# Late tokens and queries turned by the DMA queue, weight conversions by half tiles, and a new written-out order

## The chip, the core and the metric

The kernel runs on one core of a Trainium2 chip. Its time is device microseconds (us) for one execution of the whole program. The engines are TensorE (PE, with its weight loads PEld), VectorE (DVE), ScalarE (ACT), GpSimd (POOL) and SyncE (SP); each works through its own list of instructions in order and waits for the others by semaphores. SP computes nothing: it issues DMAs, and ACT and POOL issue some as well, between their own instructions.

## What is computed

Block-sparse attention over 4 batches, 8 heads, 768 tokens of width 64, and then an MLP with a PReLU on the 3072 tokens of width 512:

```python
scores = np.matmul(q, k.transpose(0, 1, 3, 2)) / np.sqrt(64)
# blocks of 32 tokens; a query block sees its neighbours, the first and the last block, 3 drawn blocks;
# the first and the last query block see everything
mask = (abs(blk_i - blk_j) <= 1) | (blk_i == 0) | (blk_j == 0) | (blk_i == 23) | (blk_j == 23) | drawn
attn = softmax(np.where(mask, scores, -1e9))
x = (attn @ v).transpose(0, 2, 1, 3).reshape(3072, 512)
h = x @ w_in                                   # 512 x 2048
g = np.maximum(h, 0.0) + alpha * np.minimum(h, 0.0)
out = g @ w_out                                # 2048 x 512
```

The MLP's weights arrive as 64-bit floats and have to be converted on the chip. Products are made with operands split into an fp16 high part and an fp16 low part (three fp16 products stand for one fp32 product).

## The kernel before, in words

**Units.** Batch b has six query tiles t of 128 tokens; tile 5 holds the dense blocks. A unit is one tile with four of the eight heads (c = 0 or 1). A unit makes scores `s` on PE, the exponent `e` (DVE L811 or L825, then ACT), fp16 high and low parts of the probabilities `p` by rows in a buffer `ph`, and SP turns these with DMA transposes (L867, L871) into `pt`; PE then makes the weighted values `a` (L713). Keys are turned the same way (L579).

**Queries and tokens.** Queries (`qf`) are turned on PE: four 128x128 transposes (L508) into PSUM, then a high part by ACT or DVE and a low part by DVE (L444) from PSUM into `qt`. When both units of a tile have their `a`, DVE multiplies by the reciprocal sums (L875, into `xf`), PE turns the tile with four transposes (`emit_x_pe`, L883), and ACT or DVE (L592, L594) and DVE (L899) write the high and low parts into `x`.

**MLP.** Two tiles of x are a chunk of 256 tokens; chunks M0 to M11, of which M6 to M11 belong to batches 2 and 3. An up-product (L1307, 24 matmuls) makes `h`; the activation makes `g`, its high part `gh` and low part `gl`; a down-product (L1368, 12 matmuls) adds into the two `o` tiles. Batch 0 and its first chunk work in fp32 ("wide", L1331, activation at L1337 and L1338). At the end of a chunk ACT scales the two tiles (`emit_out`, L1378) and SP stores them.

**Weights.** A tile f of 128 rows of w_in or w_out is loaded raw into space that is later `wo`'s (or, at the end, into idle buffers `x` and `vr`), and three instructions make fp32 of it: N1 (L1159, DVE), N2 (L1166 on DVE, or a byte move at L1164 on ACT), N3 (L1171, DVE). They work on pairs of tiles (128x1024). After them come scaling and splitting on ACT, DVE and POOL (L436, L446, L447).

**Order.** Every step is recorded as an operation with its dependencies; the string ORDER says, for each place, which operation comes next and on which engine (an operation's number and the letter of its engine). Buffers are given out in the order of that string. Nothing is decided at run time but the waits.

```python
LQW = ({"ACT": 0.45, "SP": 0.35}, {"ACT": 0.45}, {"POOL": 1.0}, {"POOL": 1.0, "ACT": 0.45})[W_ACT]
MAX4 = {"DVE": (0.42, 0), "ACT": 0.65, "POOL": 0.8}
LOW3 = {"DVE": (0.72, 0), "POOL": (0.72, 1.15)}
```

These give the engines that an operation may stand on; LQW is the list for the loads of weights.

Of the kernel before, what the change touches and what calls it, by code (L numbers as in the profile page):

```python
# [18 lines left out]
P = 128  # L19
# [27 lines left out]
W_ACT = 1  # L47
WIDE = 1
TB0, TB1 = ["o", "s"], ["s"]
# [14 lines left out]
01G2aA2eP03V02G00G0AV0EG2kA04G08G2pP09V06V07G33S2ZS2cP3GA3HP2jA0IP2dV2bA2gP2iS2nP2hV0KA0LV3IA32S34A2sS2qA2tA2rS0DG0MV2fA3JG0CA3KG2lP2mA3LG2oA0BV3MG3SP  # L64
35P3ZV3aA36V0NV43S37P38V3hG3iG3DA3jG3kG46G47G48G2uP2vV44P3TV3UA49G3bV2YS3VV2wP3mP3cA2xV2-G3dP2yV0WA3tV3WA3XP4UG3eV3nV4VG4WG45A4FP3YA2+G3uA3vV4sA3oA3pV
39G4MV3wA3xP3qA3+V0OA0SA4GV4HA3yV4IV4NA4XG4vG4ZP4OV0XV4wG4xG4yG5HG3rP5IG5JG4tP0YV4JA4KP4gV4PA4uV3BV4QP4aV3sA2XS3NG3OG0PV0QV4LA3PG3QG52P4hA4iV4AG4bA4cV
3RS5KG4RA0JV4jA4kP4dA4eP59V3lS0RV0qP0rP53V5jG30A5kG5AA5BV3CV54A55V4oV5CA5DP4BG3fP0ZV3gP5EA5MP0TV3zP0UV0VV3-P5gS4ES5NV4CG4lA56A5TV5OA5PV0HG4DG0aA4fV5UA
40V5lG4YA57P5VV41P3AV5hP5QA5mG05G42V0sP0tP0eA5iA5RP5sP3FV4SP4TP4mP7CA0FG0iA5WA65G5SV4nP5bV5XP58A0mA66G0bV0cV5tV5zV0dV4pV4qP67G68G7FG5YV7GG5-A6AP5+V4rA
6WP60A61P0fV0gV6aP0hV0uP1FA5uA1GA0vP5vV7DP0jV6XV6HV0kA6BV6CA0lV1LA6eP0wP31G0nV62A0oV5wA5xP6DV6IA0pV6EA6JV6FP6KA7HG1HV6bV0xP7IG7EA7OP2zG1KA6fV4zG4-G4+G
0yV0zP1IA1JV50G1QA51S6iP5FP0-V0GA6mP7PV7dG5nG1PA7VV5yA5oG5pG5qG1zP6PV5GP7eG7fG6VV7gG7QA7WA7iP7XV7YA7RV7SA1MV7TP1NV1OV5LA5ZP6YA6GA7ZP6jV5aP1-P6qP1RV1SV  # L70
1TV1UA80S6gA1+P7jV6nV6cA0+G10G1VA7UA81P6uP7aA7pV7kA7lV5cV5rS63P1ZA1aA7mA7nP6LP1WV7qA7rV69ABAA82A1XV1YV7oA20P83P6ZG1bV5dP64P1cV1dV1fA6MA6vV6dG7JG8CV84P
# [1449 lines left out]
```

## Time and profile before

| | |
|---|---|
| median of 3 runs | 778.02 us (777.37 to 780.0) |
| the profiled execution | 781.22 us, of which the span of its instructions is 778.5 us |
| PE busy | 727.4 us, 93% |
| DVE busy | 529.8 us, 68% |
| ACT busy | 324.4 us, 42% |
| POOL busy | 490.9 us, 63% |

The profiled execution is one execution of the program with the hardware profiler on; its time is 2.7 us more than its span, and 3.2 us above the median of the three runs without it. Busy time is the time in which an engine has an instruction under way; what the engine waits for is seen in the chain of waits and in the idle time before an instruction.

### The profile page before, as it was taken

How to read it: one execution, taken by the hardware profiler on the slowest of the kernel's cores; microseconds unless marked ns; L12 is line 12 of the kernel's file. 1: busy time of each engine (PE TensorE's matmuls, PEld its weight loads, DVE VectorE, ACT ScalarE, POOL GpSimd, SP SyncE). 2: the span in 40 equal slices, each digit the busy share in tenths (PEclk: the TensorE clock that was granted, in tenths of full speed). 3: DMA queues.
4: the chain of work that ended last, by engine and by line, in shares of the span. 5: the costliest groups of instructions: out<-in, count | busy, mean ns of one | idle time of the engine just before them, and what ended most of it. 6: DMA issues, size and time to landing. Idle time of an engine off the chain costs nothing.

```text
span 778.5 us, 25844 instructions
## 1 busy us (share of the span) xinstructions
PE 727.4 (93%) x10417; PEld 501.2 (64%) x10417; DVE 529.8 (68%) x1240; ACT 324.4 (42%) x765; POOL 490.9 (63%) x854
## 2 busy tenths in 40 slices
PE   4867997899999979999999799999999999999997
PEld 3645875656766656666776467576766677566764
DVE  4776899999748885867857456686676664665321
ACT  2532524565325434455535344355452443352211
POOL 4888676377779864468766576477586786233121
PEclk9987998999999989999999899999999999999999
DMA  9979886746685978967679869657897768345100
GB/s 225 277 192 302 238 213 172 147 90 161 152 184 119 166 151 152 188 137 157 144 210 167 156 131 164 161 109 144 134 202 163 142 130 163 62 89 85 36 1 27
DMA packets 241607, 117.63 MB, mean 151 GB/s; under 512 B 194496, under 2 KB 227920, under 8 KB 241488
## 3 DMA queue, kind: packets, MB, share of 16 engines
q1 hardware_dynamic: 196224, 64.46, 45.1%
q10 hardware_dynamic: 39600, 33.69, 16.2%
q0 software_dynamic: 5664, 17.84, 9.0%
q8 instruction: 81, 1.33, 0.8%
q14 instruction: 38, 0.31, 0.2%
HBM read 71.91 MB, written 12.58 MB: 109 GB/s over the span
## 4 chain that ended last, share of the span: by engine, by line
PE 80%; DVE 8%; issue 5%; POOL 3%; DMA 2%; ACTq 1%; POOLq 1%; ACT 0%; SPq 0%; DVEq 0%
PE o L1368 31%; PE h L1307 29%; PE s L713 7%; PE a L713 6%; DVE wo L1171 1%; PE h L1331 1%; DVE wo L1166 1%; ACTq L464 1%; POOL keys L708 1%; PE s L883 1%; PE s L508 1%; DVE wo L1159 1%; DMA vf<-in_k_dram 1%; DVE e L811 1%; DVE ph L438 1%
## 5 line engine op out<-in xcount | busy, mean ns | idle before, releaser
L1307 PE MATMUL h<-x,wi 128*128 128x256 f16 x2112 | 247.1, 274 | 1.3 <-DVE g L1338 1.3
L1368 PE MATMUL o<-wo,gh 128*128 128x512 f16 x768 | 230.3, 382 | 0.0
L1307 PEld LDWEIGHTS <-wi 128*128 128x128 f16 x2112 | 204.4, 99 | 36.2 <-issue 4.6
L1324 POOL TENSOR_TENSOR gl<-g,gh 128x512 f16<-128x512 f32 x88 | 105.7, 1205 | 158.1 <-ACT gh L1319 149.5
L1368 PE MATMUL o<-wo,gl 128*128 128x512 f16 x384 | 146.3, 381 | 0.0
L708 POOL COPY keys<-keys 128x128 f16 (+1 forms) x480 | 129.8, 319 | 15.4 <-PE s L713 11.3
L818 ACT ACTIVATE e<-e,smalls 128x256 f32<-128x256 f32 x160 | 80.2, 502 | 127.8 <-DVE smalls L811 121.8
L1368 PEld LDWEIGHTS <-gh 128*128 128x128 f16 x768 | 72.6, 99 | 75.4 <-issue 4.8
L1313 DVE SCALAR_TENSOR_TENSOR g<-h,am 128x512 f32<-128x512 f32 x88 | 60.4, 686 | 78.0 <-PE h L1307 60.8
L1319 ACT CAST gh<-g 128x512 f16<-128x512 f32 x88 | 53.7, 612 | 133.6 <-DVE g L1314 96.2
L665 POOL DMA_INDIRECT vr<-scr,vidx x80 | 83.3, 1042 | 24.7 <-issue 16.4
L713 PE MATMUL s<-keys,qt 64*32 64x192 f16 (+5 forms) x2376 | 77.6, 271 | 10.9 <-ACT pt L436 4.7
L811 DVE CUSTOM_DVE_ANT_0 e<-s,bias,smalls 128x256 f32<-128x256 f32 x120 | 54.1, 478 | 25.4 <-PE s L713 22.3
L713 PEld LDWEIGHTS <-pt 128*32 128x32 f16 (+1 forms) x3456 | 48.8, 96 | 30.4 <-issue 23.5
L1368 PEld LDWEIGHTS <-gl 128*128 128x128 f16 x384 | 37.7, 98 | 46.0 <-issue 1.1
L1314 DVE SCALAR_TENSOR_TENSOR g<-h,g 128x512 f32<-128x512 f32 x88 | 60.8, 691 | 3.0
L444 DVE SCALAR_TENSOR_TENSOR ph<-e,ph 128x512 f16<-128x512 f32 (+1 forms) x56 | 50.3, 903 | 11.9 <-ACT ph L436 11.5
L713 PE MATMUL a<-vr,pt 128*32 128x64 f16 (+1 forms) x1760 | 43.2, 205 | 10.2 <-issue 6.1
L447 POOL TENSOR_TENSOR ph<-e,ph 128x512 f16<-128x512 f32 (+1 forms) x36 | 50.7, 1408 | 3.0
L436 ACT ACTIVATE ph<-e 128x512 f16<-128x512 f32 (+1 forms) x66 | 46.2, 706 | 3.6 <-DMA keys<-ph 2.3
L836 ACT ACTIVATE e<-e,smalls 128x768 f32<-128x768 f32 x32 | 29.8, 930 | 40.7 <-DVE smalls L832 40.3
L713 PE MATMUL a<-vn,pt 128*32 128x64 f16 (+1 forms) x1760 | 40.8, 205 | 5.0 <-DMA vn<-scr 4.0
(225 smaller groups left out, 933.7 us busy)
## 6 DMA issues: line engine op xcount, KB each, us to landing
vn<-scr SPq DMA_DIRECT2D x54, 192.0 KB, 4.1
wo<-in_moe_w_in_dram ACTq DMA_DIRECT2D x8, 1024.0 KB, 10.9
wo<-in_moe_w_out_dram ACTq DMA_DIRECT2D x12, 512.0 KB, 4.1
vn<-scr ACTq DMA_DIRECT2D x26, 192.0 KB, 4.1
vf<-in_v_dram SPq DMA_DIRECT2D x14, 256.0 KB, 3.4
vf<-in_k_dram SPq DMA_DIRECT2D x24, 128.0 KB
qf<-in_q_dram SPq DMA_DIRECT2D x12, 256.0 KB, 5.5
scr<-v SPq DMA_DIRECT2D x11, 256.0 KB, 3.0
```

Source lines behind the costliest of these rows:

```text
L447: nc.gpsimd.tensor_tensor(dst, tmp, hi, ALU.subtract)
L665: nc.gpsimd.indirect_dma_start(dst[:n], None, T["scr", b].rearrange("s h a -> s (h a)"), bass.IndirectOffsetOnAxis(ap=vidx[:n, i : i + 1], ...
L708: nc.gpsimd.tensor_copy(kr[:, :, r], kt[:, :, bass.ds(i * HB2, HB2)])
L713: nc.tensor.matmul(dst, lhs, rhs, start=start, stop=False, skip_group_check=True)
L811: nc.vector.tensor_tensor_reduce(e_view(u, h // 2)[:, h % 2, :], T["sp", u, h], bias[:, t], scale=T["cs", b, t][:, c : c + 1], scalar=3.0e ...
L818: nc.scalar.activation(e, e, AF.Exp, bias=T["nm", u, h], scale=-1.0, accum_out=su_of(u, h))
L1307: nc.tensor.matmul(h[:, i, :], win(k, f, ct), x[:, l, ct, :], start=(m == 0), stop=(m == len(terms) - 1))
L1313: nc.vector.scalar_tensor_tensor(g, ph, 0.0, a2, ALU.min, ALU.mult)
L1314: nc.vector.scalar_tensor_tensor(g, ph, GSCALE, g, ALU.mult, ALU.add)
L1319: nc.scalar.copy(T["gh", c, j], g)
L1324: nc.gpsimd.tensor_tensor(T["gl", c, j], g, T["gh", c, j], ALU.subtract)
L1368: nc.tensor.matmul(T["o", c, t], g[:, i, t * P : (t + 1) * P], wout(w, f), start=(f == 0 and m == 0), stop=(f == NF - 1 and m == 2),)
```

## The change

Six things change.

1. Batch 3's six query tiles (`Q_T`) and the twelve x tiles of batches 2 and 3 (`X_T`) are no longer turned on PE. DVE, ACT or POOL writes the high part and DVE or POOL the low part by rows into a `ph` buffer, and SP issues one DMA transpose for each tile.
2. N1, N2 and N3 work on single tiles (128x512) in place of pairs. Of N1 and N3 there are now 32 each (18 before), of N2 15 on ACT and 17 on DVE (4 and 14 before).
3. The first chunk's activation is a Relu with scale -1 on ACT, from PSUM, and two DVE instructions of 128x256 for each up-product, in place of two DVE instructions of 128x512. `emit_alpha` has one instruction more.
4. Loads of weights may be issued by SP as well as by ACT: 16 of 24 now stand on SP.
5. The last three down-products of the last chunk are made by token tile, and tile t = 1's output is scaled and stored in two halves.
6. ORDER is another one: 2535 operations in place of 2480, and most stand elsewhere.

```diff
-W_ACT = 1
+W_ACT = 0
+Q_T = {(3, t) for t in range(6)}
+X_T = {(b, t) for b in (2, 3) for t in range(6)}
...
 ORDER = """
-01G2aA2eP03V02G00G0AV0EG2kA04G08G2pP09V06V07G33S2ZS2cP3GA3HP2jA0IP2dV2bA2gP2iS2nP2hV0KA0LV3IA32S34A2sS2qA2tA2rS0DG0MV2fA3JG0CA3KG2lP2mA3LG2oA0BV3MG3SP
+3DS03V06V08G0IP04V09V05G00G02G01G3wS0BV0AV0FG0DG3GP3FS3NS3RP07G3KP3LV3HA3xP3ES3IP3JV3MA3VA3PP0GA3yV3QV3OS3TP3XA3zG3-G3UA4jS3kA3SA3+G3iA40G46P4kP4LG4lA
...
+    def by_rows(nb):
+        return phs[nb.slot].rearrange("p a b c -> p (a b c)")[:, : 2 * HQ * P]
+
+    def emit_q_n_hi(e, b, t, nb):
+        T["qn", b, t] = by_rows(nb)
+        times(e, T["qn", b, t][:, : HQ * P], T["qf", b, t].rearrange("p h d -> p (h d)"), T["sq", b, t])
+
+    def emit_q_n_lo(e, b, t):
+        src, nat = T["qf", b, t].rearrange("p h d -> p (h d)"), T["qn", b, t]
+        rest(e, nat[:, HQ * P :], src, T["sq", b, t], nat[:, : HQ * P], src)
+
+    def emit_q_t(b, t):
+        T["qt", b, t] = wt("qt", [P, H, P], F16)
+        nc.sync.dma_start_transpose(T["qt", b, t], T["qn", b, t])
...
+    def emit_x_n_hi(e, b, t, nb):
+        T["xn", b, t] = by_rows(nb)
+        src, dst = T["xf", b, t].rearrange("p h d -> p (h d)"), T["xn", b, t][:, : HQ * P]
+        if e == "POOL":
+            nc.gpsimd.tensor_copy(dst, src)
+        else:
+            copy(e, dst, src)
+
+    def emit_x_n_lo(e, b, t):
+        nat = T["xn", b, t]
+        eng_of[e].tensor_tensor(nat[:, HQ * P :], T["xf", b, t].rearrange("p h d -> p (h d)"), nat[:, : HQ * P], ALU.subtract)
+
+    def emit_x_t(b, t):
+        nc.sync.dma_start_transpose(x_part(b, t), T["xn", b, t])
...
+        if (b, t) in X_T:
+            nb = plan.buf("ph")
+            o = plan.op(p - X_UP, MAX4, lambda e: emit_x_n_hi(e, b, t, nb), [o], [nb], [fb])
+            o = plan.op(p - X_UP, {"DVE": (0.7, 0), "POOL": (0, 1.2)}, lambda e: emit_x_n_lo(e, b, t), [o], [], [nb, fb])
+            o_x[b, t] = plan.op(p - X_UP, {"SP": 1.3}, lambda: emit_x_t(b, t), [o], [xbuf[cc]], [nb], dma=1.55)
+            return
...
         nc.vector.tensor_scalar(am1, am0, GSCALE, None, ALU.mult)
+        nc.vector.tensor_scalar(am0, am0, -1.0, None, ALU.mult)
...
-    def emit_n1(name, fs):
-        r, low, d, byte = raw_of(name, fs)
+    def emit_n1(name, fs, i):
+        r, low, d, byte = raw_of(name, fs, i)
         nc.vector.tensor_scalar(d, r, 3, 0x3FFFFFFF, ALU.logical_shift_left, ALU.bitwise_and)
...
-        o = plan.op(p, {"DVE": (0.4 * n, 0)}, lambda: emit_n1(name, fs), o + free, [], use)
-        o = plan.op(p, {"ACT": 1.27 * n, "DVE": (0.65 * n, 0)}, lambda e: emit_n2(e, name, fs), [o], [], use)
-        return plan.op(p, {"DVE": (0.65 * n, 0)}, lambda: emit_n3(name, fs), [o], [], use)
+        last, ld = [], o
+        for i in range(n):
+            o = plan.op(p, {"DVE": (0.4, 0)}, lambda i=i: emit_n1(name, fs, i), (ld if name == "wi" else ld[i : i + 1]) + free, [], use)
+            o = plan.op(p, {"ACT": 1.27, "DVE": (0.65, 0)}, lambda e, i=i: emit_n2(e, name, fs, i), [o], [], use)
+            last = [plan.op(p, {"DVE": (0.65, 0)}, lambda i=i: emit_n3(name, fs, i), [o] + last, [], use)]
+        return last[0]
...
-    def emit_act_wide(j, gb):
-        h = T["h", 0, j]
-        g = T["g", 0, j] = wt(gb.pool, [P, 2, W2], F32)
-        a2 = am0[:, 2 * j : 2 * j + 2].unsqueeze(2).broadcast_to([P, 2, W2])
-        nc.vector.scalar_tensor_tensor(g, h, 0.0, a2, ALU.min, ALU.mult)
-        nc.vector.tensor_tensor(g, h, g, ALU.add)
+    def emit_act_neg(j, gb):
+        T["g", 0, j] = wt(gb.pool, [P, 2, W2], F32)
+        nc.scalar.activation(T["g", 0, j], T["h", 0, j], AF.Relu, scale=-1.0)
+
+    def emit_act_wide(j):
+        h, g = T["h", 0, j], T["g", 0, j]
+        for i in range(2):
+            nc.vector.scalar_tensor_tensor(g[:, i], g[:, i], am0[:, 2 * j + i : 2 * j + i + 1], h[:, i], ALU.mult, ALU.add)
...
+                if c == len(chunks) - 1 and j >= NG - 3:
+                    o = [plan.op(p, {"PE": 1.3}, lambda j=j, t=t: emit_down_half(c, j, t), d + fin[t], [], [hbs[j], lbs[j], obufs[t]]) for t in range(2)]
+                    fin = [[x] for x in o]
+                    continue
```

The order of instructions is shown at three places. The first is the start of DVE's list. `sf`, `bq`, `dd` and `btab` belong to the mask of the drawn blocks, `vpick`, `vrow` and `vidx` to the indices of the gathered values, and `spack` (L365 before, L368 after) packs the block numbers that POOL then reads into its registers. Before:

```order
L321 TENSOR_SCALAR wi<-rawp 1x72
L330 TENSOR_TENSOR dd<-sf,bq 128x15
L331 TENSOR_TENSOR dd<-dd 128x15
...
L409 SCALAR_TENSOR_TENSOR vpick<-vpick,vrow 128x20
L410 TENSOR_SCALAR vidx<-vpick,vrow 128x20
L365 SCALAR_TENSOR_TENSOR spack<-wi 1x30
L594 COPY keys<-s_109 128x4x128
```

After:

```order
L324 TENSOR_SCALAR wi<-rawp 1x72
L368 SCALAR_TENSOR_TENSOR spack<-wi 1x30
L327 TENSOR_SCALAR vpick<-rawp 128x60
L328 MEMSET vpick 32x60
...
L413 TENSOR_SCALAR vidx<-vpick,vrow 128x20
L346 SCALAR_TENSOR_TENSOR dtab<-bcol,sf,dtab 128x24 x3
L333 TENSOR_TENSOR dd<-sf,bq 128x15
...
L612 COPY keys<-s_109 128x4x128
```

The packing moves from behind the mask and the indices to the place directly behind the block numbers; the mask now comes last.

The second place is DVE's list where w_out is converted and the first chunk's activations stand between the conversions. `wo` is w_out's space, `vf_70` a `g` of the first chunk, `h_113` its up-product, `am_153` alpha's table. Before:

```order
L1159 TENSOR_SCALAR wo<-wo 128x1024
L1166 SCALAR_TENSOR_TENSOR wo<-wo 128x1024
L1171 SCALAR_TENSOR_TENSOR wo<-wo 128x1024
L1337 SCALAR_TENSOR_TENSOR vf_70<-h_113,am_153 128x512
L1338 TENSOR_TENSOR vf_70<-h_113,vf_70 128x512
```

After:

```order
L1206 TENSOR_SCALAR wo<-wo 128x512
L1213 SCALAR_TENSOR_TENSOR wo<-wo 128x512
L1218 SCALAR_TENSOR_TENSOR wo<-wo 128x512
L1390 SCALAR_TENSOR_TENSOR vf_70<-vf_70,am_153,h_113 128x256 x2
L829 ISA e_75,smalls<-s_111,bias,cs_140 128x256
...
L1206 TENSOR_SCALAR wo<-wo 128x512 x2
L1213 SCALAR_TENSOR_TENSOR wo<-wo 128x512
L1218 SCALAR_TENSOR_TENSOR wo<-wo 128x512 x2
```

A set of N1, N2, N3 is of half the size and there are twice as many; in the last rows one of two N2 is missing, it stands on ACT. Softmax rows (`e_75`) and activations come between smaller pieces.

The third place is PE's list around the last chunk's second x tile. `a_112` is the weighted values from which that tile is made, `xf_83` the tile, `x_84` and `x_86` the x of the last chunk (before and after), `gh_104`, `gh_103`, `gh_102` high parts of the chunk before. Before:

```order
L713 MATMUL a_112<-v_97,pt_79 128x64
L1307 LDWEIGHTS wi
L1307 MATMUL h_114<-x_86,wi 128x256
...
L883 MATMUL s_111<-ident,xf_83 128x128 x4
L1368 LDWEIGHTS gh_104
...
L1368 MATMUL o_116<-wo,gl_106 128x512
L1307 LDWEIGHTS wi
L1307 MATMUL h_113<-x_84,wi 128x256
```

After:

```order
L731 MATMUL a_112<-v_94,pt_80 128x64
L1420 LDWEIGHTS gh_104
...
L1420 LDWEIGHTS gh_103
...
L1420 LDWEIGHTS gh_102
...
L1357 LDWEIGHTS wi
L1357 MATMUL h_114<-x_86,wi 128x256
```

The four transposes (`s_111<-ident,xf_83`) are gone from PE, and three down-products in place of an up-product, the transposes and a down-product stand between the last weighted values and the first up-product that reads the new tile. Meanwhile the tile goes through DVE, ACT or POOL and then SP, whose list at this place reads, after:

```order
L889 DMA_TRANSPOSE pt_80<-ph_137 128x6x128
L889 DMA_TRANSPOSE pt_79<-ph_137 128x6x128
L922 DMA_TRANSPOSE x_86<-ph_134 128x8x128
L922 DMA_TRANSPOSE x_86<-ph_135 128x8x128
L467 DMA out_dram<-g_88 128x512
```

The two x tiles are turned behind the last transposes of dense probabilities. At the very end of ACT's list (not shown) the two halves of tile t = 1 are scaled first, then tile t = 0, and then ACT issues the store of t = 0.

## Rows read from the trace of the kernel before

**Rows 1.** Windows: length; PE, PEld, DVE, ACT, POOL busy us; clock, DMA share, GB/s.
```profile
0.00:92.00 92.00, 66.92 (x874) 51.03 (x875) 62.31 (x171) 34.98 (x91) 68.34 (x191) 0.91 0.94 246
92.00:148.00 56.00, 47.78 (x692) 37.47 (x691) 54.41 (x91) 23.89 (x49) 35.84 (x26) 0.94 0.74 192
...
430.00:720.00 290.00, 282.72 (x4462) 191.26 (x4447) 184.42 (x461) 121.27 (x290) 177.29 (x290) 0.99 0.71 135
```

**Rows 2.** Chain of waits in the stretch 92 to 148, shares by line.
```profile
by line: DVE wo L1171 20.8%; DVE wo L1166 19.4%; DVE wo L1159 13.9%; issue 9.0%; DVE e L811 6.1%; PE s L713 4.3%; DVE e L825 3.8%; PE a L713 3.4%; DVE xf L875 2.5%; DVE g L1338 2.5%; DVE vf L1337 2.2%; DVE g L1337 2.2%; DVE ph L444 1.7%; DV
```

**Rows 3.** Chain of waits from 448 to 458: start us, us, what.
```profile
448.89 0.44 PE s L883 x4
449.33 2.59 PE o L1368 x12
...
456.53 0.59 PE s L508 x4
```

**Rows 4.** DVE's groups by line and shape, 92 to 148: busy us, mean ns | idle.
```profile
L1171 DVE SCALAR_TENSOR_TENSOR wo<-wo 128x1024 int32<-128x1024 int32 x5 | 11.2, 2250 | 0.2
L1166 DVE SCALAR_TENSOR_TENSOR wo<-wo 128x1024 int32<-128x1024 int32 x5 | 9.6, 1913 | 0.1
L1159 DVE TENSOR_SCALAR wo<-wo 128x1024 int32<-128x1024 int32 x5 | 6.6, 1311 | 0.0
...
L875 DVE TENSOR_TENSOR xf<-a,smalls 128x512 f32<-128x512 f32 x3 | 2.1, 687 | 0.5 <-PE a L713 0.5
...
L899 DVE TENSOR_TENSOR x<-o,x 128x512 f16<-128x512 f32 x2 | 1.4, 682 | 0.0
```

**Rows 5.** DVE timeline from 72: start us, us, instruction.
```profile
72.36 0.68 DVE L1159 TENSOR_SCALAR wi<-wo 128x1024 int32<-128x1024 int32 x1
73.08 1.23 DVE L1166 SCALAR_TENSOR_TENSOR wi<-wo,wi 128x1024 int32<-128x1024 int32 x1
74.34 1.23 DVE L1171 SCALAR_TENSOR_TENSOR wi<-wo,wi 128x1024 int32<-128x1024 int32 x1
```

**Rows 6.** DVE timeline from 141: conversions of single tiles.
```profile
141.46 0.43 DVE L1159 TENSOR_SCALAR wo<-vr 128x512 int32<-128x512 int32 x1
141.80 0.69 DVE L1166 SCALAR_TENSOR_TENSOR wo<-x,wo 128x512 int32<-128x512 int32 x1
```

**Rows 7.** DVE timeline from 87: the first chunk's activation.
```profile
87.89 0.69 DVE L1338 TENSOR_TENSOR g<-h,g 128x512 f32<-128x512 f32 x1
88.50 0.68 DVE L1337 SCALAR_TENSOR_TENSOR g<-h,am 128x512 f32<-128x512 f32 x1
89.22 0.69 DVE L1338 TENSOR_TENSOR g<-h,g 128x512 f32<-128x512 f32 x1
```

**Rows 8.** POOL and DVE timelines from 97: two instructions that run at once.
```profile
97.85 2.00 POOL L447 TENSOR_TENSOR gl<-g,gh 128x512 f16<-128x512 f32 x1
...
98.87 2.06 DVE L1171 SCALAR_TENSOR_TENSOR wo<-wo 128x1024 int32<-128x1024 int32 x1
```

**Rows 9.** SP's transposes of probabilities (line L867): duration min/median/max, time to landing.
```profile
L867 SPq DMA_TRANSPOSE pt<-ph x60: 1231/1258/3727, 237.4 to 674.6; - x60
...
DMA to landing us min/median/max: 3.0/4.8/10.6
```

**Rows 10.** Timeline of the start; start us, us, instruction.
```profile
13.73 0.17 DVE L365 SCALAR_TENSOR_TENSOR spack<-wi 1x30 int32<-1x30 int32 x1
...
17.48 0.65 POOL L708 COPY keys<-keys 128x64 f32 x1
```

**Rows 11.** ACT timeline from 60; in brackets the idle time before and its releaser.
```profile
60.49 4.58 ACTq L464 DMA_DIRECT2D wo<-in_moe_w_in_dram  x1
65.11 0.51 ACT L818 ACTIVATE e<-e,smalls 128x256 f32<-128x256 f32 x1 [4.68 <-issue]
```

**Rows 12.** Timeline of the end.
```profile
773.53 1.27 ACT L1378 ACTIVATE g<-o,smalls 128x512 f32<-128x512 f32 x2 [5.61 <-PE o L1368]
```

**Rows 13.** PE timeline, 437 to 444.
```profile
442.92 0.27 PE L713 MATMUL a<-vr,pt 128*32 128x64 f16 x5 [5.17 <-issue]
```

More of the change, by code (lines that the diff above doesn't have):

```diff
@@ L68 @@
[L68 to L71, printed above, removed]
@@ L114 @@
+d7Pd4Vd5Ad6Gd8PdCPd9VdAAdBGdDPdHPdEVdFAdGGdIPdMPdJVdKAdLGdNPdRPdSPdOVdPAdQGdTPdUPdVPdWPdZAdbAdXAdaSdcSdYA
 """
@@ L1166, in emit_n2, with emit_n3 @@
             nc.vector.scalar_tensor_tensor(d, low, 29, d, ALU.logical_shift_right, ALU.bitwise_or)
-        T["mask", name, fs] = 7 - (1 << 30) if e == "ACT" else -(1 << 30)
-    def emit_n3(name, fs):
-        r, low, d, byte = raw_of(name, fs)
-        nc.vector.scalar_tensor_tensor(d, r, T["mask", name, fs], d, ALU.bitwise_and, ALU.bitwise_or)
+        T["mask", name, fs, i] = 7 - (1 << 30) if e == "ACT" else -(1 << 30)
+    def emit_n3(name, fs, i):
+        r, low, d, byte = raw_of(name, fs, i)
+        nc.vector.scalar_tensor_tensor(d, r, T["mask", name, fs, i], d, ALU.bitwise_and, ALU.bitwise_or)
     def emit_w_sq(name, fs, tb, first, last):
@@ L1357, in emit_fs, with emit_down @@
         nc.vector.reciprocal(T["fs", b], t1)
-    def emit_down(c, j):
+    def emit_down(c, j, ts=(0, 1)):
         if j == 0:
@@ L1365, in emit_down @@
             f = 2 * j + i
-            for t in range(2):
+            for t in ts:
                 for m, (g, w) in enumerate(((gh, 0), (gh, 1), (gl, 0))):
@@ L1374, in emit_down, with emit_down_half @@
                     )
+    def emit_down_half(c, j, t):
+        emit_down(c, j, (t,))
     def emit_out(c, t):
@@ L1378, in emit_out, with emit_out_half, emit_store, emit_store_half @@
         nc.scalar.activation(T["ob", c, t], T["o", c, t], AF.Copy, scale=T["fs", chunks[c][0]])
-    def emit_store(e, c, t):
+    def emit_out_half(e, c, t, x):
+        if x == 0:
+            T["ob", c, t] = wt("g", [P, DM], F32)
+        y = slice(x * DM // 2, (x + 1) * DM // 2)
+        times(e, T["ob", c, t][:, y], T["o", c, t][:, y], T["fs", chunks[c][0]])
+    def emit_store(e, c, t, y=slice(0, None)):
         b, i = chunks[c]
         for a, z, s in q_rows(b, 2 * i + t):
-            load(e, out[b * S + s : b * S + s + z - a], T["ob", c, t][a:z])
+            load(e, out[b * S + s : b * S + s + z - a, y], T["ob", c, t][a:z, y])
+    def emit_store_half(e, c, t, x):
+        emit_store(e, c, t, slice(x * DM // 2, (x + 1) * DM // 2))
     o_fs = {}
@@ L1413, in moe @@
                     last = o
-                    o = plan.op(p - MOE_BOOST, {"DVE": 1.47}, lambda j=j, gb=gb[j]: emit_act_wide(j, gb), [o, o_al], [gb[j]], [hb])
+                    o = plan.op(p - MOE_BOOST, {"ACT": 0.6}, lambda j=j, gb=gb[j]: emit_act_neg(j, gb), [o], [gb[j]], [hb])
+                    o = plan.op(p - MOE_BOOST, {"DVE": 0.85}, lambda j=j: emit_act_wide(j), [o, o_al], [], [gb[j], hb])
                 else:
@@ L1432, in moe @@
             ob = plan.buf("g")
-            o = plan.op(stop - MOE_BOOST, {"ACT": 0.58}, lambda t=t: emit_out(c, t), [downs[-1], o_fs[b]], [ob], [obuf])
+            if fin[t] and t == 1:
+                for x in range(2):
+                    o = plan.op(stop - MOE_BOOST, {"ACT": 0.38, "DVE": 0.4}, lambda e, x=x: emit_out_half(e, c, 1, x), fin[1] + [o_fs[b]], [ob] if x == 0 else [], [obuf] + ([ob] if x else []))
+                    plan.op(stop - MOE_BOOST, LQ, lambda e, x=x: emit_store_half(e, c, 1, x), [o], [], [ob], dma=0.8, n=1 + (2 * ci + 1 == TS))
+                continue
+            o = plan.op(stop - MOE_BOOST, {"ACT": 0.58}, lambda t=t: emit_out(c, t), [downs[-1], o_fs[b]] + fin[t], [ob], [obuf])
             plan.op(stop - MOE_BOOST, LQ, lambda e, t=t: emit_store(e, c, t), [o], [], [ob], dma=0.8, n=1 + (2 * ci + t == TS))
```

115 lines of the change are left out of this document (63 added, 52 removed).

## The prediction

> **What bounds the kernel now.** I read the windows first. From 430 to 720 PE is busy 282.72 of 290 us at a granted clock of 0.99 [rows 1]: in the middle and late stages PE is the bound, so an instruction that leaves PE there is worth about its own length, and a transfer off PE costs nothing as long as it lands in time. In the first 148 us it is another matter. From 0 to 92 PE is busy 66.92 of 92 us, so 25.1 us are lost there. From 92 to 148 PE is busy 47.78 of 56 and DVE 54.41, which leaves DVE 1.6 us of rest [rows 1]: there DVE is the bound. The chain of waits in that stretch says the same by line: DVE's three conversion lines carry 20.8, 19.4 and 13.9%, together 54% of it, and PE's L713 7.7% [rows 2]. Where the chain is DVE's, PE's busy time is no price; the price is what DVE's list gets shorter or longer by.
>
> The sum is made against the profiled execution, 781.22 us (span 778.5 and 2.7 us outside it). That stands 3.2 us above the median of 778.02, so the forecast is the median less the sum of the terms.
>
> **Term 1, transposes off PE.** 18 sets of four transposes leave PE (12 of x, 6 of queries), all of batches 2 and 3. In the chain a set takes 0.44 us for x and 0.59 for a query tile [rows 3]; these are steps along the chain, in which nothing else of PE runs. 12 × 0.44 + 6 × 0.59 = 8.8 us, and where a set also makes PE change from its fp16 work nothing more is seen behind it: the next down-product takes its usual 2.59 [rows 3]. I take 9.0, the ends being 7.9 (18 × 0.44) and 10.6 (18 × 0.59).
>
> What takes their place: high and low parts written from `xf` or `qf`, on the same engines as before or on POOL, and 18 transposes on SP. From 430 to 720 DVE is busy 184.42 of 290 us (64%), ACT 121.27 (42%) and POOL 177.29 (61%) [rows 1], so these lists have room. A DVE part costs 0.68 us as the low part did [rows 4]. I cost them at nothing for PE, under the cover of PE's own products; without that cover an x tile costs its latency, which is term 4.
>
> **Term 2, the start.** DVE's packing of the block numbers runs at 13.73, behind the mask and the indices; POOL loads its registers from it, and its first copies of gathered keys start at 17.48, 3.75 us later [rows 10]. After, the packing stands second in DVE's list, ahead of the 28 small instructions of mask and indices. Taken at its own length of 0.17 each [rows 10] these are 4.8 us, at 0.25 each 7 us; but POOL's copies also need the keys, which arrive by DMA; 3 us is what I let through. Bounds: 0 (the keys are late anyway) and 7 (all of it). Against it stands that more weight loads are issued on SP; one such issue took 4.58 us of ACT and left ACT idle 4.68 [rows 11]. If SP meets one ahead of a load of keys or values, up to 4.6 us are lost here: bounds +4.6 to -7, value -3.
>
> **Term 3, the stretch 92 to 148.** In whole pairs a set steps 0.72 (73.08 - 72.36), 1.26 (74.34 - 73.08) and 1.26 us where nothing disturbs it [rows 5]: 3.24. For single tiles N1 steps 0.34 (141.80 - 141.46) and N2 and N3 about 0.60 (by the step of an equally long activation instruction, 88.50 - 87.89 = 0.61) [rows 6, 7]. Before, the stretch holds five whole sets and four single ones (4 N1, 2 N2, 4 N3): 5 × 3.24 + 4 × 0.34 + 6 × 0.60 = 21.2 us. After, DVE has 13 N1, 6 N2 and 15 N3 there: 13 × 0.34 + 21 × 0.60 = 17.0 us, since seven more halves of N2 go to ACT, busy 23.89 of 56 [rows 1]. Gain 4.2. The first chunk's activation: before, two steps, 0.61 and 0.72 = 1.33 [rows 7]; after, two instructions of half the length, 0.45 each as the 0.43 of a 512-element instruction is the nearest short one [rows 6], with the Relu on ACT ahead of them: 0.90. Five of these stand in the stretch: 5 × 0.43 = 2.1. Together -6.3, if the time that DVE's conversions lose to disturbance stays as it is.
>
> That loss is large. The five whole sets took 1311, 1913 and 2250 ns of mean [rows 4], 27.4 us together, where undisturbed steps make 16.2: some 11.2 us, 0.75 for each of 15 instructions, while POOL is busy 35.84 us of the 56 [rows 1]. An N3 that starts at 98.87 lasts 2.06 us beside a POOL subtraction of 2.00 that started at 97.85 [rows 8]. If the loss goes with the time that both engines run, it shrinks or stays with halves; if every instruction waits once, however short, 34 halves lose 34 × 0.75 = 25.5 in place of 11.2, that is +14.3, and term 3 turns to +8. I take the first, because N1's mean of 1.31 against 0.68 is a smaller loss (0.63) than N3's of 2.25 against 1.23 (1.02): the shorter instruction loses less. Ends: -8 to +8.
>
> The Trainium skill, "SBUF — State Buffer", section "SBUF: two separate sides", says that DVE and GpSimd share a pair of ports as an exclusive lock, held for the length of an instruction, so that the loser stands still. This trace agrees in kind (2.06 for 1.23 in the row named above); the rule speaks against the change, since more and shorter instructions on DVE mean more turns at the lock, and by it term 3 would be the +8.
>
> **Term 4, x tiles in time.** Each of the six late chunks now needs, from the last weighted values to its first up-product: the multiplication 0.69, high part and low part 0.68 each, and a transpose that lands 4.8 us after issue in the median, from 3.0 to 10.6 [rows 4, 9]: 6.9 us, from 5.1 to 12.7. By the order the cover on PE at the last chunk is three down-products of 2.59 [rows 3], 7.8 us; at the others two or three products and a stage of scores, much the same. So it is in time by 0.9 us in the median, and late by 4.9 where a transpose takes the longest. On SP it stands behind one to three transposes of 1.26 us each [rows 9], so some are late; I take 0.5 us for each of six chunks, +3. Bounds 0 and 6 × 4.9 = 29.
>
> **Term 5, the end.** The last output is scaled 1.27 us for two tiles, right after the last product [rows 12]. By token tile, t = 1 would be finished earlier; but in ACT's list tile t = 0 stands behind t = 1's two halves, and its store behind that, on ACT. One wait takes the place of the other; I take 0, bounds ±0.6, half of the 1.27.
>
> **Sum.** -9.0 - 3 - 6.3 + 3 + 0 = -15.3, which from the median of 778.0 gives about 762.5 us (781.2 - 15.3 = 765.9 for an execution with a profile).
>
> **The rivals.**
>
> B: only the transposes count. DVE's conversions lose as much as they gain and the start is set by the keys: -9 + 3 = -6 with the late tiles of term 4, -9 without, so 769 to 772. For it: 0.94 of the DMA share in the first 92 us [rows 1], which says that loads are late there.
>
> C: more goes than I count. ACT's 4.68 us behind a weight load [rows 11] and PE's 5.17 us without a releaser at 437 to 443 [rows 13] stand in the order before; with loads on SP and another order both may be gone: -15.3 - 4.7 - 5.2 = -25.2, about 752. Against it: the next order may have such a place elsewhere.
>
> D: each short instruction waits as a long one (term 3 at +8). Then -9 - 3 + 8 + 3 = -1, 777, no change.
>
> E, slower: SP's queue. One mechanism, at the six late chunks' tokens: the transposes stand on SP behind those of probabilities, which wait for their own low parts, and land near the longest 10.6. 4.9 us late at each of six chunks is 29 in place of 3: -9 - 3 - 6.3 + 29 = +11, 789. It decides from 3.6 us of lateness for each chunk on (21.4 / 6 in place of 0.5), where the gain is used up. For it: SP sets nothing aside for x, and a transpose held SP up to 3.7 us [rows 9]. Against it: the median of 4.8 leaves room.
>
> **How the numbers follow.** A measurement of this kernel tells about 0.3% (2.3 us) from no change. My forecast with both gains has 0.45 at 762.5 (its own range 756 to 769), B 0.22, C 0.15, D 0.07, E 0.11. So faster holds 0.82, the same 0.07, slower 0.11. The range goes from C's end, 751, to D's, 777, and leaves E and what is below C out.
>
> **What would show it.** In the profile after: no L883 or L508 of batch 3 on PE, and PE's busy time some 9 us less; POOL's first key copies at about 14.5; the stretch of conversions with means near 0.34 and 0.6 plus no more than half of 0.75 each, and ending some 6 us earlier than the start alone explains. Wrong would be: halves with the same excess as pairs (D), PE idle before the first up-product of M6 to M11 with SP's transposes as the releaser (E), or a DVE that is idle in the first 148 us because raw weights come late through SP (then terms 2 and 3 are not paid out, as in B).

## The result and the profile after

The changed kernel takes 756.26 us (median of 4 runs, 753.37 to 760.11), the kernel before on the same chip 778.5 (777.37 to 780.0). The ratio is 0.9716, interval 0.9669 to 0.9763: 2.4 to 3.3% faster. The forecast was 762.5, a ratio of 0.98. The measured time lies inside the range of the forecast (751 to 777) and 6.2 us below its value, and 0.98 lies outside the measured interval.

To see where the time went, both spans are cut at the same three events: the first wide up-product of chunk M0, the first fp16 up-product, and the last up-product. Windows of the kernel before (length, then PE, PEld, DVE, ACT, POOL busy, granted clock, DMA share, GB/s):

```profile
0.00:75.10 75.10, 50.02 (x733) 36.29 (x733) 48.60 (x144) 26.23 (x76) 57.43 (x173) 0.89 0.95 249
75.10:136.60 61.50, 55.36 (x739) 44.54 (x732) 56.92 (x91) 26.14 (x53) 42.83 (x42) 0.94 0.80 211
136.60:765.40 628.80, 613.94 (x8921) 416.80 (x8918) 422.84 (x1005) 270.12 (x633) 389.49 (x640) 0.99 0.69 136
765.40:778.50 13.10, 8.04 (x39) 3.53 (x36) 1.38 (x2) 1.89 (x3) 1.16 (x1) 0.90 0.12 40
```

The same windows of the changed kernel:

```profile
0.00:67.50 67.50, 44.61 (x734) 33.12 (x734) 44.58 (x155) 31.68 (x85) 44.86 (x155) 0.87 0.97 260
67.50:126.30 58.80, 54.71 (x739) 44.26 (x731) 52.34 (x115) 33.18 (x65) 44.00 (x50) 0.94 0.88 242
126.30:744.60 618.30, 604.34 (x8851) 408.03 (x8847) 421.94 (x1001) 270.06 (x635) 394.46 (x636) 0.99 0.77 146
744.60:758.30 13.70, 8.02 (x39) 3.49 (x36) 1.38 (x2) 2.04 (x4) 1.16 (x1) 0.98 0.12 38
```

| stretch | before | after | difference | forecast |
|---|---|---|---|---|
| to the first wide up-product | 75.1 | 67.5 | -7.6 | -3 (term 2) |
| to the first fp16 up-product | 61.5 | 58.8 | -2.7 | -6.3 (term 3) |
| to the last up-product | 628.8 | 618.3 | -10.5 | -9 + 3 (terms 1, 4) |
| to the end | 13.1 | 13.7 | +0.6 | 0 (term 5) |
| span | 778.5 | 758.3 | -20.2 | -15.3 |

Of the 7.6 us of the first stretch, PE's idle time gives 2.2 (25.1 to 22.9). The other 5.4 are busy time: 733 and 734 matmuls take 50.0 and 44.6 us; why they ran shorter was not settled. What PE waits for at the start is not the same either (us in total, times, longest): the wait for keys gets shorter, and one for alpha is new. Before, then after:

```profile
PE o L585 <- DMA vf<-in_k_dram: 7.8, 4, 6.3
```

```profile
PE h L1174 <- DMA wi<-in_moe_alpha_dram: 5.0, 1, 5.0
PE o L603 <- DMA vf<-in_k_dram: 1.8, 1, 1.8
```

In the third stretch PE is busy 9.6 us less. The two lines that turn tiles take 12.9 us of PE there in place of 24.1, 11.2 less, of which other groups take back 1.6. PE's idle time goes only from 14.9 to 14.0 us. The wait of 5.2 us that [rows 13] shows is gone (none of its kind there is longer than 1.6), but PE now waits for the last conversions of w_out (L1230 multiplies each converted tile with itself). The longest of PE's waits in the third stretch, before and after:

```profile
PE a L713 <- issue: 7.1, 3, 5.2
```

```profile
PE o L1230 <- DVE wo L1218: 4.6, 3, 2.4
```

The x tiles are in time. The view of SP's x transposes, and the group of up-products in the page (idle time last):

```profile
L922 SPq DMA_TRANSPOSE x<-ph x12: 1232/1249/1642, 422.8 to 705.1; - x12
DMA to landing us min/median/max: 3.1/3.2/3.6
```

```profile
L1357 PE MATMUL h<-x,wi 128*128 128x256 f16 x2112 | 248.7, 275 | 0.0
```

All twelve land after 3.1 to 3.6 us, not the 4.8 in the median of [rows 9], and no up-product waits for a turned tile.

DVE's groups between the two up-products show what halves cost; they answer to [rows 4]:

```profile
L1218 DVE SCALAR_TENSOR_TENSOR wo<-wo 128x512 int32<-128x512 int32 x12 | 11.8, 1009 | 0.3
...
L1206 DVE TENSOR_SCALAR wo<-wo 128x512 int32<-128x512 int32 x12 | 5.3, 462 | 0.0
...
L1213 DVE SCALAR_TENSOR_TENSOR wo<-wo 128x512 int32<-128x512 int32 x6 | 4.4, 740 | 0.1
L1390 DVE SCALAR_TENSOR_TENSOR g<-g,am,h 128x256 f32<-128x256 f32 x9 | 3.9, 474 | 1.4 <-ACT g L1385 1.4
```

N1, N2 and N3 on half the data take 462, 740 and 1009 ns, where pairs took 1311, 1913 and 2250. For the Relu on ACT DVE waits 1.4 us before these nine instructions and 0.6 us before the six others of this kind in the stretch.

The conversions run on past the first fp16 up-product. The last one, before and after (DVE's timelines):

```profile
145.61 0.69 DVE L1171 SCALAR_TENSOR_TENSOR wo<-vr,wo 128x512 int32<-128x512 int32 x1
```

```profile
137.93 1.05 DVE L1218 SCALAR_TENSOR_TENSOR wo<-vr,wo 128x512 int32<-128x512 int32 x1
```

They end at 146.3 and 139.0, that is 71.2 and 71.5 us behind the first wide up-product: no earlier than the start alone explains. Up to there DVE is busy 66.5 us before and 64.9 after. A single half can still lose much beside POOL, as this N3 does (0.69 us long in the row at 145.61):

```profile
132.56 2.44 POOL L450 TENSOR_TENSOR wi<-wi 128x1024 f16<-128x1024 f32 x1
```

```profile
132.94 2.60 DVE L1218 SCALAR_TENSOR_TENSOR wo<-vr,wo 128x512 int32<-128x512 int32 x1
```

At the start (DVE's and POOL's timelines) the block numbers are packed at 4.17, 9.6 us earlier than in [rows 10], yet POOL's first copies begin only 3.9 us earlier and wait for a copy of queries:

```profile
4.17 0.18 DVE L368 SCALAR_TENSOR_TENSOR spack<-wi 1x30 int32<-1x30 int32 x1
```

```profile
13.56 0.61 POOL L726 COPY keys<-keys 128x64 f32 x3 [2.95 <-DVE qt L612]
```

The end went as forecast: tile t = 0 is scaled behind the halves of t = 1, and ACT's store of it is issued last.

```profile
752.70 0.84 ACT L439 ACTIVATE g<-o,smalls 128x256 f32<-128x256 f32 x2 [5.60 <-PE o L1420]
...
753.43 0.69 ACT L1433 ACTIVATE g<-o,smalls 128x512 f32<-128x512 f32 x1
754.15 0.36 ACTq L467 DMA_DIRECT2D out_dram<-g  x1
```

### The profile page after: what moved, and what is told of

Read it like the earlier page. It is cut to its first block, busy times and chain, and to the rows that moved or that the text cites. A ratio compares the mean times of both kernels' runs of the same rounds, so it can differ in the third digit from the quotient of the medians.

```text
span 758.3 us, 25828 instructions
## 1 busy us (share of the span) xinstructions
PE 711.7 (94%) x10345; PEld 488.9 (64%) x10345; DVE 520.2 (69%) x1271; ACT 337.0 (44%) x787; POOL 484.5 (64%) x842
## 3 DMA queue, kind: packets, MB, share of 16 engines
q10 hardware_dynamic: 24672, 21.63, 10.5%
## 4 chain that ended last, share of the span: by engine, by line
PE 77%; DVE 5%; DMA 3%; issue 2%; POOL 1%; ACT 0%; SPq 0%; POOLq 0%; ACTq 0%
PE o L1420 32%; PE h L1357 29%; PE a L731 6%; PE s L731 6%; DVE wo L1218 1%; DMA pt<-ph 1%; DMA vr<-scr,vidx 1%; PE s L511 1%; PE h L1381 1%; DVE wo L1206 1%; PE s L901 1%; PE s L568 0%; PE o L1261 0%; DVE v L447 0%; PE s L495 0%
## 5 line engine op out<-in xcount | busy, mean ns | idle before, releaser
L726 POOL COPY keys<-keys 128x128 f16 (+1 forms) x480 | 133.9, 327 | 12.9 <-PE s L731 6.5
L683 POOL DMA_INDIRECT vr<-scr,vidx x80 | 78.1, 977 | 18.4 <-issue 15.6
L731 PE MATMUL s<-keys,qt 64*32 64x192 f16 (+5 forms) x2376 | 72.3, 265 | 4.2 <-DVE smalls L843 3.1
L447 DVE SCALAR_TENSOR_TENSOR ph<-e,ph 128x512 f16<-128x512 f32 (+1 forms) x61 | 56.3, 925 | 6.8 <-ACT ph L439 5.7
L731 PE MATMUL a<-vr,pt 128*32 128x64 f16 (+1 forms) x1760 | 41.0, 203 | 12.8 <-DMA vr<-scr,vidx 9.8
L449 POOL TENSOR_SCALAR e<-e 128x512 f32<-128x512 f32 (+1 forms) x31 | 24.4, 786 | 39.7 <-ACT ph L439 25.7
L450 POOL TENSOR_TENSOR ph<-e,ph 128x512 f16<-128x512 f32 (+1 forms) x31 | 43.0, 1388 | 2.6
L843 DVE CUSTOM_DVE_ANT_0 e<-s,dbias,smalls 128x384 f32<-128x384 f32 x48 | 28.8, 612 | 19.1 <-PE s L731 18.9
```

What stands on the lines that cost most here:

```text
L447: nc.vector.scalar_tensor_tensor(dst, src, scale, hi, ALU.mult, ALU.subtract)
L683: nc.gpsimd.indirect_dma_start(dst[:n], None, T["scr", b].rearrange("s h a -> s (h a)"), bass.IndirectOffsetOnAxis(ap=vidx[:n, i : i + 1], ...
L726: nc.gpsimd.tensor_copy(kr[:, :, r], kt[:, :, bass.ds(i * HB2, HB2)])
L731: nc.tensor.matmul(dst, lhs, rhs, start=start, stop=False, skip_group_check=True)
```

## The experiments

Ten variants ran and the changed kernel twice more, four at a time on one chip, each beside the kernel before; groups 2 and 3 ran on the same chip. These chips ran the kernel before in 797 to 800 us, so mostly ratios to it, or profiles of one group of four, are compared. A window is that of one execution: the first stretch of the changed kernel was 67.5, 67.9 and 69.1 us long in three of them, and 70.5 in pe_turn, whose order differs only behind it. The ratios of the table are estimates with a 95% interval, not quotients of the medians beside them.

| kernel | group | median | before | ratio, interval |
|---|---|---|---|---|
| pe_turn | 1 | 781.76 | 797.12 | 0.9766 (0.9704 to 0.9827) |
| pack_late | 1 | 767.82 | 797.12 | 0.9611 (0.9569 to 0.9653) |
| b_halves | 1 | 800.8 | 797.12 | 1.0034 (0.9996 to 1.0072) |
| n2_dve | 1 | 778.1 | 797.12 | 0.9730 (0.9673 to 0.9787) |
| after_again | 2 | 769.44 | 800.05 | 0.9619 (0.9583 to 0.9656) |
| loads_act | 2 | 781.74 | 800.05 | 0.9768 (0.9727 to 0.9809) |
| act_old | 2 | 774.21 | 800.05 | 0.9684 (0.9641 to 0.9726) |
| b_pack | 2 | 796.8 | 800.05 | 0.9961 (0.9926 to 0.9996) |
| old_pe | 3 | 801.65 | 798.5 | 1.0063 (1.0034 to 1.0091) |
| old_turn | 3 | 816.43 | 798.5 | 1.0214 (1.0167 to 1.0262) |
| after_third | 3 | 771.53 | 798.5 | 0.9656 (0.9616 to 0.9697) |
| b_loads | 3 | 797.98 | 798.5 | 1.0001 (0.9970 to 1.0032) |

### The turn on PE again (pe_turn)

```diff
-Q_T = {(3, t) for t in range(6)}
-X_T = {(b, t) for b in (2, 3) for t in range(6)}
+Q_T = set()
+X_T = set()
 ORDER = """   # high part's place -> PE, low part's -> ACT, SP's -> DVE; x sets behind the next product
-...MqG...MrV...MsS...
+...MqP...MrA...MsV...
```

> The changed kernel, with the 18 tiles turned on PE again (each set of four transposes behind the next product, high part on ACT, low part on DVE). If term 1 holds, PE's busy time from the first fp16 up-product to the last grows by about 9 us and the time by 6 to 9 us against the changed kernel, to 762 to 766. If the late stage gained from the new order and not from the transposes, the time stays within 3 us of the changed kernel.

In its group the changed kernel stands in pack_late (below: the same but for one small instruction). The ratio is 0.9766 to 0.9611, 1.6% or some 13 us. The third stretch of pe_turn and of pack_late, in this order:

```profile
130.00:768.90 638.90, 616.43 (x8922) 418.15 (x8919) 419.79 (x1002) 274.70 (x645) 379.47 (x623) 0.99 0.67 134
```

```profile
126.90:752.20 625.30, 605.78 (x8854) 408.16 (x8847) 419.02 (x1001) 269.96 (x635) 390.24 (x636) 0.99 0.76 144
```

PE is busy 10.7 us more and idle 3 us more, so the time grows by more than the 6 to 9 us expected: the price of 18 sets is near what term 1 said, and 3 us of waiting come on top. The places on PE were not tuned, so these 3 us may belong to them.

### The packing, late in the new kernel and early in the old (pack_late, b_pack)

```diff
 # pack_late, in the changed kernel (06 is the packing, 0A the mask)
-3DS03V06V08G0IP04V09V05G00G02G01G3wS0BV0AV0FG
+3DS03V08G0IP04V09V05G00G02G01G3wS0BV0AV06V0FG
 # b_pack, in the kernel before
-01G2aA2eP03V02G00G0AV0EG2kA04G08G2pP09V06V07G
+01G2aA2eP03V06V02G00G0AV0EG2kA04G08G2pP09V07G
```

> The changed kernel, with the packing of the block numbers behind the mask and the indices again on DVE. If the start was gained by the early packing, the first wide up-product starts 3 us or more later than at 67.5 and the time is 759 to 763. If the start is set by keys and weights instead, the first copies of gathered keys on POOL start later but the first wide up-product does not move by more than 1 us and the time stays near 756.

> The kernel before, with the packing of the block numbers directly behind the numbers themselves on DVE; nothing else moves. If the packing sets the start, POOL's first copies of gathered keys begin about 3 us earlier than at 17.48 and the time falls by 2 to 3 us. If keys and queries set the start anyway, the time stays within 1 us.

In the changed kernel the late packing costs nothing that the ratios show (0.9611; the kernel as it is stood at 0.9619 and 0.9656, each with 0.4% either way): packed at 9.73, the copies still start at 13.45 and wait for the same copy of queries, in its POOL timeline:

```profile
13.45 0.78 POOL L735 COPY keys<-keys 128x64 f32 x4 [3.04 <-DVE qt L621]
```

In the kernel before, the early packing gains 0.39% (0.04 to 0.74), 3.1 us. There it was what the copies waited for; they start at 15.55 in place of 17.48, 1.9 us earlier and not the 3 expected, and then wait for keys:

```profile
15.55 1.49 POOL L711 COPY keys<-keys 128x64 f32 x8 [0.78 <-DVE keys L597]
```

### Halves alone (b_halves)

```diff
-        nc.vector.tensor_scalar(d, r, 3, 0x3FFFFFFF, ALU.logical_shift_left, ALU.bitwise_and)
+        for a in range(0, r.shape[1], 512):
+            nc.vector.tensor_scalar(d[:, a : a + 512], r[:, a : a + 512], 3, 0x3FFFFFFF, ALU.logical_shift_left, ALU.bitwise_and)
 # N2 and N3 on DVE in the same way
```

> The kernel before, with every N1, N2 and N3 of DVE on 1024 elements written as two of 512 at the same place; nothing else moves. If the time lost beside POOL goes with the length, each half of N3 in w_out's stretch takes about half of 2250 ns and the time stays within 3 us of 778. If every instruction waits once, halves of N3 there take some 1600 ns and the stretch and the time grow by about 14 us.

1.0034 (0.9996 to 1.0072), 2.7 us and not 14. DVE's groups between the two up-products:

```profile
L1174 DVE SCALAR_TENSOR_TENSOR wo<-wo 128x512 int32<-128x512 int32 x10 | 11.4, 1178 | 0.0
L1182 DVE SCALAR_TENSOR_TENSOR wo<-wo 128x512 int32<-128x512 int32 x12 | 9.7, 848 | 0.0
L1164 DVE TENSOR_SCALAR wo<-wo 128x512 int32<-128x512 int32 x12 | 9.6, 837 | 0.0
```

Two halves of N1, N2 and N3 take 2 × (0.837 + 1.178 + 0.848) = 5.73 us; a pair's set took 1.31 + 1.91 + 2.25 = 5.47 [rows 4]. For the same data between the same two up-products the kernel before has these groups, and its N2 of [rows 4], 29.3 us together where the halves take 30.7:

```profile
L1171 DVE SCALAR_TENSOR_TENSOR wo<-wo 128x1024 int32<-128x1024 int32 x6 | 12.5, 2086 | 0.2
L1159 DVE TENSOR_SCALAR wo<-wo 128x1024 int32<-128x1024 int32 x6 | 7.2, 1207 | 0.0
```

In sum the loss goes with the length, nearly, though a half N2 takes more than half of its pair's time and a half N3 less. By rival D the 17 more instructions would have lost 0.75 us each, 12.8 in place of 1.4: D is out, and halving by itself gains nothing.

### Three reliefs taken back, one at a time (n2_dve, loads_act, act_old)

```diff
 # n2_dve: the 15 N2 that stand on ACT
-0kA0PA0aA...
+0kV0PV0aV...
 # loads_act: the 16 loads of weights that stand on SP
-0RS0YS0fS...
+0RA0YA0fA...
 # act_old
-        nc.scalar.activation(T["g", 0, j], T["h", 0, j], AF.Relu, scale=-1.0)
+        nc.scalar.activation(T["g", 0, j][:, 0, :1], T["h", 0, j][:, 0, :1], AF.Relu, scale=-1.0)
...
-        for i in range(2):
-            nc.vector.scalar_tensor_tensor(g[:, i], g[:, i], am0[:, 2 * j + i : 2 * j + i + 1], h[:, i], ALU.mult, ALU.add)
+        nc.vector.scalar_tensor_tensor(g, h, 0.0, a2, ALU.min, ALU.mult)
+        nc.vector.tensor_tensor(g, h, g, ALU.subtract)
```

> The changed kernel, with all 32 N2 on DVE (15 of them stand on ACT in it). If DVE sets the end of the conversions, 15 more instructions of 0.60 to 0.74 us put 7 to 11 us on DVE's list, and the time grows by 5 us or more, to 761 and above. If DVE has become idle enough before the first fp16 up-product, the time stays within 2.5 us of 756.

> The changed kernel, with all 24 loads of weights issued by ACT at the same places of the order (16 of them stand on SP in it). If moving them to SP took a block of 4 to 5 us out of ACT's first 70 us, the first wide up-product starts 2 us or more later than in the changed kernel and the time grows by 2 to 5 us. If a load blocks SP as it blocks ACT, or the block in the kernel before hung on its place in the order, the time stays within 2 us.

> The changed kernel, with the first chunk's activation as two DVE instructions of 128x512 again (the Relu on ACT is left at one element for each partition). DVE gets 8 times about 0.45 us more and ACT 8 times 0.6 less. If DVE sets the end of the conversions, the time grows by 2 to 4 us. If DVE has rest there by now, it stays within 1.5 us.

N2 on DVE: 0.9730 against 0.9611, 1.2% or 10 us. Its first two windows are 72.1 and 62.7 us long, those of pack_late 68.2 and 58.7. Loads on ACT: 0.9768 against 0.9619, 1.5% or 12 us, more than expected; first two windows, as after_again and as loads_act:

```profile
0.00:67.90 67.90, 46.35 (x733) 34.58 (x733) 44.56 (x155) 32.03 (x85) 44.51 (x155) 0.85 0.98 259
67.90:125.90 58.00, 54.60 (x738) 44.02 (x730) 53.01 (x115) 33.33 (x65) 44.46 (x50) 0.97 0.88 245
```

```profile
0.00:72.00 72.00, 46.30 (x733) 35.22 (x733) 44.14 (x155) 31.97 (x85) 43.82 (x155) 0.86 0.91 244
72.00:134.40 62.40, 56.17 (x739) 44.88 (x732) 51.43 (x115) 33.26 (x65) 42.73 (x50) 0.92 0.80 208
```

8.5 us are lost in front of the first fp16 up-product, with the DMA share down from 0.98 and 0.88 to 0.91 and 0.80: loads start later. The third weight load is issued at 40.31 in loads_act; in the changed kernel the third and the fourth are issued by SP at 30.66 and 34.08:

```profile
40.31 0.38 ACTq L476 DMA_DIRECT2D wo<-in_moe_w_in_dram  x1
```

```profile
30.66 0.43 SPq L467 DMA_DIRECT2D wo<-in_moe_w_in_dram  x1
...
34.08 0.44 SPq L467 DMA_DIRECT2D wo<-in_moe_w_in_dram  x1
```

The old activation: 0.9684 against 0.9619, about 5 us, just beyond the uncertainty of the two (0.0056). The windows of n2_dve and loads_act show that DVE's list and the times at which loads are issued still set the first 126 us; of act_old only the time is compared.

### The loads alone in the kernel before (b_loads)

```diff
-W_ACT = 1
+W_ACT = 0
 # the 16 loads that SP issues in the changed kernel: engine letter A -> S
```

> The kernel before, with the 16 loads of weights issued by SP that SP issues in the changed kernel; nothing else moves. If ACT's blocks behind weight loads (4.58 us at 60.5) were what delayed the first wide up-product, it starts 3 us or more earlier and the time falls by 3 to 5 us. If SP's own queue delays the loads by as much, no change.

1.0001 (0.9970 to 1.0032): no change in the time, though in the profile the first wide up-product starts at 72.0 (75.1 in the kernel before, on another chip). The same move that is worth 12 us in the new order is worth nothing that shows in the old one. It says little of rival C, because the load that held ACT for 4.58 us [rows 11] is not among the 16 and still holds it here:

```profile
59.20 3.69 ACTq L467 DMA_DIRECT2D wo<-in_moe_w_in_dram  x1
62.94 0.51 ACT L821 ACTIVATE e<-e,smalls 128x256 f32<-128x256 f32 x1 [3.63 <-issue]
```

In the changed kernel no weight load holds ACT longer than 1.98 us (at 66.68), and with all loads on ACT (loads_act) none longer than 2.30 (at 71.23). So the block went with the new order, not with the move to SP; what it cost was not tested.

### All edits in the old order (old_pe, old_turn)

The changed code with an ORDER built from the old one: each operation where its counterpart stood; where one became two, side by side, on the engines of the new order. In old_pe the 18 tiles stay on PE, in old_turn SP turns them.

> The changed code in the order of the kernel before, tiles turned on PE: halves, 15 of N2 on ACT, the Relu on ACT, 16 loads of weights on SP and the last products by tile, each where its counterpart stood. If these edits gain by themselves, the time falls by 10 us or more against the kernel before (the removal of single ones from the changed kernel cost 5 to 12 us each). If they only gain in an order made for them, the time stays within 4 us of the kernel before.

> The same with the 18 tiles turned by SP, in the old order (each transpose where the low part stood; five tiles moved as far as buffers demand). If the turn gains what PE's transposes took, it is 9 to 13 us faster than its twin on PE. If x is late in the old order, where the first up-product follows soon, the gain is below 5 us. The rest to the changed kernel is the order's share.

> The changed kernel as it is, beside the three others of this chip: 0.96 to 0.975 of the kernel before.

| | ratio to before |
|---|---|
| old order, all edits but the turn | 1.0063 (1.0034 to 1.0091) |
| old order, all edits | 1.0214 (1.0167 to 1.0262) |
| new order, all edits | 0.9656 (0.9616 to 0.9697) |

In the old order the edits cost 0.6% and the turn another 1.5%, where a gain was expected, of 9 to 13 us or of less than 5; against this filling of the old order the new one is worth 5.6% on the same code. The third stretch of old_pe and of old_turn:

```profile
141.30:785.20 643.90, 621.09 (x8926) 419.89 (x8919) 410.02 (x1001) 273.18 (x638) 389.12 (x640) 0.98 0.66 132
```

```profile
142.20:806.30 664.10, 620.48 (x8849) 412.46 (x8846) 410.63 (x990) 272.62 (x638) 400.21 (x653) 0.98 0.70 135
```

PE is idle 22.8 us in the one and 43.6 in the other. A part of this is rival E at work. PE's waits for what SP turns in that stretch, in old_turn and then in old_pe, and one row of PE's timeline in old_turn:

```profile
PE h L1363 <- DMA x<-ph: 4.8, 3, 2.7
PE a L737 <- DMA pt<-ph: 4.3, 2, 3.4
```

```profile
PE a L737 <- DMA pt<-ph: 0.7, 2, 0.6
```

```profile
769.93 1.25 PE L1363 MATMUL h<-x,wi 128*128 128x256 f16 x10 [2.67 <-DMA x<-ph]
```

Up-products wait 4.8 us for turned tiles, where in the changed kernel they wait for none, and weighted values wait 4.3 us for turned probabilities in place of 0.7. Together that is 8.4 of the 20.8 us more idle time; the rest is spread over waits of at most 3.5 us more each and was not settled. PE's busy time stays at 620 us without the 72 transposes: the same up-products take 251.6 us of it in place of 245.1, and from 560 to 720 the granted clock is 0.97 (old_pe: 1.00). The old order was filled by rule and not tuned, so another filling of it may do better than 1.0214.

## Why the prediction was right, and where not

**What bounds the kernel.** Right in its stages: PE in the middle and late stages (9.6 us less work there, 10.5 less time), DVE early (in n2_dve 15 more instructions on its list cost 10 us).

**Term 1.** -9.0 forecast, 9.6 us of PE's busy time measured (11.2 on the lines that turn tiles) and 10.7 when it was put back. The size came from the two chain pieces of [rows 3].

**Term 2.** -3 forecast, -7.6 measured, and for a reason that I did not give. In the kernel before, the packing alone is worth the 3 us (b_pack: 3.1), but in the changed kernel it is worth none that shows, since a copy of queries sets the copies there. What shortened the start is known in part: taking the loads back from SP costs 4.1 us to the first wide up-product and taking N2 back from ACT 3.9, each in a single execution. In the old order the same two reliefs leave it at 74.2 (old_pe), so they do not shorten it as much without the new order; what the order does by itself was not measured. The load issues on SP stood in the term as a risk; they were a gain.

**Term 3.** -6.3 forecast, -2.7 measured between the two up-products. That the time lost beside POOL goes with the length was nearly right in sum. What failed is that the gain was taken in full: between the two up-products PE was busy 55.36 of 61.5 us, so 6.1 us was all that there was to gain, and the next waits (dense scores for DVE's sums, 3.1 us in one piece) came before that. I read DVE's 54.41 of 56 and did not ask how far below it PE stood. Nor did DVE's list get shorter by what I took off it: up to the last conversion it is busy 1.5 us less and not 6.3, since the new order puts other work there (two low parts of values, 3.3 us, among it). The sign that the prediction named, conversions that end some 6 us earlier than the start explains, is missing (71.2 and 71.5 us), and PE waits 4.6 us for the last of them behind the first fp16 up-product, where it waited 0.8 before. The prediction's "seven more" halves of N2 on ACT are five by its own counts (2 of 14 before, 7 of 13 after); its sum does not use the word.

By the Trainium skill's "SBUF — State Buffer", section "SBUF: two separate sides", the loser of a turn at the shared ports stands still for the other's whole instruction. The trace agrees for single instructions (a half N3 of 2.60 us beside a POOL subtraction of 2.44). That term 3 would be the +8 by this rule was my own step, since the rule does not say how often a turn is lost: the loss per data nearly stayed (5.73 us for 5.47), and more turns at the lock did not mean much more time here.

**Term 4.** +3 forecast, none measured. The landing time was taken from the transposes of probabilities (median 4.8), those of x land in 3.1 to 3.6. That the risk was real is shown by old_turn, where x is late: the order, not the edit, decides.

**Term 5.** 0 forecast, +0.6 in the span: the one wait did take the place of the other.

**The rivals.** B is out (start and conversions gave 10.3 us of the span together). C came nearest to the number (752), and both waits that it named are gone. But PE's idle time in the third stretch falls by 0.9 us only, since the 4.6 us for the last conversions took the place of PE's 5.2, as the objection to C said, and what ACT's block at the start cost is not shown. D is out by b_halves. E did not occur, by the landing times; old_turn shows a part of it. The lateness at which E uses up the gain is (9 + 3 + 6.3) / 6 = 3.05 us for each chunk by the sum's own terms, not the 3.6 given.

So the total is right within 5 us of the span because terms 2 and 4 erred to one side and term 3 to the other, which is luck. That the terms can be added was a weak point: taken back one at a time from the changed kernel, the turn, the loads, N2 and the Relu cost 13, 12, 10 and 5 us, 40 in all, of a gain of some 29 on those chips; in the old order all of them together gain nothing.

## What to carry to other kernels

An edit that frees an engine pays only if the order lets the work behind it move up: here the same code is 2.1% slower than before in the old order, as filled here, and 3.4% faster in the new one, so price the edits and the order together, and test an edit in the order in which it will stand. Where one engine is the bound of a stretch, read how far the next one is below it before a gain is taken in full. For a transfer moved to another queue, take the landing time at the place where it will stand, and look at what else that queue issues.

## What the runs showed of the hardware

The chips differ: the kernel before ran in 778.5 us on the first, in 797.12 on that of group 1, and in 800.05 and 798.5 on that of groups 2 and 3; the ratio of the same changed kernel was 0.9716 on the first and 0.9619 and 0.9656 in groups 2 and 3. Such differences are as large as most of the edits studied here, so a time from one group is not set beside a time from another. The traces show where they lie: the first two stretches of the changed kernel are 67.5 and 58.8 us long on the first chip and 67.9 and 58.0 in group 2, the third 618.3 and 633.0, of which PE is idle 14.0 and 22.4. Of the waits there, those of weighted values that no releaser is shown for grow most, from 3.0 us in 2 pieces to 10.2 in 14. The reason stays open.
